# Attention loads placed nearer to their use, v loaded last, attention pairs moved over the slots, and one gather of gates moved to the first stretch

## The chip, the cores and the metric

One Trainium2 chip, of which the kernel uses one core. The time is the device time of that core in microseconds, median of several runs. A core has a matrix engine (TensorE, PE in the profile; its weight loads are PEld), a vector engine (DVE), a scalar engine (ACT), a GpSimd engine (POOL) and a sync engine (SP) that here does little else than issue transfers (DMAs). Each engine works through its own instructions in order. Where one needs what another makes, it waits on a semaphore, and all that is behind it on that engine waits too.

## The reference

Two blocks, one behind the other. The first is a linear attention with a decay `lam` for each head, over 4 batches, 8 heads, 768 positions and 64 values for each head:

```python
for b in range(nb):                                  # blocks along the sequence
    intra = einsum('bhic,bhjc->bhij', qb, kb) * Dmask[None]       # lam ** (i - j), lower triangle
    intra = einsum('bhij,bhjd->bhid', intra, vb)
    inter = einsum('bhid,bhde->bhie', qb * lam_pow[None], kv_state)
    out[:, :, sl] = intra + inter
    kb_dec = kb * rev_pow[None]
    kv_state = lam_block * kv_state + einsum('bhsd,bhse->bhde', kb_dec, vb)
```

Its output, as 3072 tokens of 512 values, is the input x of a mixture of four experts, whose gates come from another input:

```python
p = domain_probs / (domain_probs.sum(-1, keepdims=True) + 1e-09)
for e in range(E):                                   # E = 4, w1 is 512 x 1024, w2 is 1024 x 512
    h = np.maximum(x @ w1[e], 0.0)
    out += p[:, e:e + 1] * (h @ w2[e])
```

All is float32.

## The kernel before, in words

**Tiling.** The 3072 tokens are three groups, 0 to 2, of eight chunks of 128 tokens. A chunk is one batch's 128 positions with all heads. The attention works with chunks of 128 in place of the reference's blocks of 64, two chunks (a pair, n and n + 1) at a time, so a group has four pairs. Every expert product is a fast product with seven multiplications in place of eight, nested once more, so 7 x 7 small products; their sums and differences are made by DVE, POOL and ACT.

**One pair of attention** takes four steps:

- `load`: for each chunk q and k (two DMAs each, line 142) and v (one DMA, line 137) into buffers of 128 x 512. In groups 1 and 2 these come from the common pool of 41 small buffers; a new load waits until the last reader of its buffer is done.
- `turn`: q and k of a chunk are transposed by PE into the two accumulator banks s0 and s1, ACT copies them to qT and kT, and POOL multiplies k by a decay. For the last two chunks of each batch (the function `comes_across`; all of group 2's) q and k are laid out anew through DRAM before (`trickle`, `load_across`), and DVE transposes blocks in place, qx and then kx. That is work for the list `lately`, from which the loop takes one piece in each part.
- `scores` (line 581): products of kT and qT into four banks, sp. DVE multiplies them by the decay mask (`st <- sp, s_decay`, line 589) and, but for the first chunk, scales qT (`qT <- qT, q_decay`, line 593).
- `values` (lines 625, 631, 639): the product with the state, the product of the masked scores with v, and the new state. ACT copies the result, POOL makes the pair's sums for the fast product (`pair_sums`), and DVE updates the state.

**Order.** The order of the work is written out by hand; there is no search. Group 0's attention is done in the first stretch, up to 91.9 us, with parts of the first products put between its steps by the dictionary `between` (line 1325). The main loop then runs over 12 units (group, expert), each of 7 slots. A slot has 8 parts, 0 to 7, and carries one seventh of the second product of one unit and one seventh of the first product of the next. Slots are counted through from 0; slot s belongs to unit s // 7. Groups 1 and 2 are spread over these slots: `attention` (line 684) fills a list `steps` of (slot, part, work) from the table `AT`, which has one slot for each of the eight pairs. I count them from 1 to 8: pairs 1 to 4 are group 1, at slots 7, 10, 13 and 15; pairs 5 to 8 are group 2, at slots 22, 27, 32 and 37. The list is sorted by slot and part, and the loop takes out what is due at the end of each part (line 1496).

**Queues.** Nearly all DMAs are issued by SP in program order. In each slot these are the weights of the first product one slot ahead (`feed`, part 0, `ws_in`, two buffers), weights of the second product (`feed2`, `w2t`), stores of prepared sums, the attention's loads, and the blocks of x that a later group's products read (`x_fill`, part 3 of seven slots from `FILL[g]` on). POOL's work (`chores`) is taken from a list by an estimate of how busy POOL is: one chore when the estimated time of the last has gone by. DVE's smaller pieces wait in `background` and `lately`, one of each for a part.

**Gates.** `gates` (in the first stretch) turns the probabilities into gates for all tokens. The last group needs its gates along the other axis. `turn_gates`, a chore of unit (1, 0), gathers eight columns by eight DVE copies into a small tile gn (line 490), has PE transpose it (line 491, `gp`), and stores it to DRAM.

The lines that the prediction names beyond these: 899 is the matmul of the first product (`pg`), 953 that of the second (`q`), 812 the DMA of `feed`, 911 a relu by ACT, and line 101 is the helper `tt` through which DVE and POOL additions go, so that these are told apart by their tiles.

Of the kernel before, what the change touches and what calls it, by code (L numbers as in the profile page):

```python
# [14 lines left out]
FP32 = mybir.dt.float32  # L15
# [6 lines left out]
def kernel(  # L22
# [30 lines left out]
    nc = tc.nc  # L53

    B, H, S, D = q.shape
    E, DM, F = moe_w1.shape
    NTOK, DOUT = out.shape
    P = nc.NUM_PARTITIONS
# [3 lines left out]
    CPG = 8  # L62
# [8 lines left out]
    consts = ctx.enter_context(tc.tile_pool(name="consts", bufs=1))  # L71
# [16 lines left out]
    def bank(tag, name):  # L88
        return ps.tile([P, W], FP32, name=name, tag=tag)

    def small(name):
        return pool.tile([P, W], FP32, name=name, tag="t")
# [24 lines left out]
    def token(g, half, x):  # L117
        c, b = (half, x) if g == 0 else (2 * g + x % 2, 2 * (x // 2) + half)
        return b * S + c * C
# [4 lines left out]
    def where(n):  # L124
        g, x = divmod(n, CPG)
        return (x // 4, x % 4) if g == 0 else (2 * g + x // 2 % 2, 2 * (x // 4) + x % 2)
# [3 lines left out]
    def load(n, names="qkv"):  # L130

        c, b = where(n)
        for name in names:
            x = ({"k": acc_tile, "v": w2_tile} if n < CPG else {}).get(name, small)(f"{name}n")
            src = {"q": q, "k": k, "v": v}[name][b, :, c * C:(c + 1) * C, :]
            if name == "v":
                nc.sync.dma_start(out=x[:].rearrange("p (h d) -> p h d", d=D), in_=src.rearrange("h p d -> p h d"))
            else:
                to, of = x[:].rearrange("p (i r d) -> p i r d", r=2, d=D), src.rearrange("(r i) p d -> p i r d", r=2)
                for r in range(2):  # L140
                    by = nc.scalar if n < 2 and r == 1 else nc.sync
                    by.dma_start(out=to[:, :, r], in_=of[:, :, r])
            nat[n, name] = x[:].rearrange("p (h d) -> p h d", d=D)
# [202 lines left out]
    ident = consts.tile([P, P], FP32, name="ident")  # L346
# [42 lines left out]
    def trickle(m=1):  # L389
        for _ in range(m):  # L390
            if pieces:
                pieces.pop(0)[1]()

    def comes_across(n):
        return where(n)[0] >= SECOND

    def load_across(n):
        c, b = where(n)
        for x, name in enumerate("qk"):
            t = small(f"{name}x")  # L400
            nc.sync.dma_start(
                out=t[:].rearrange("p (h c) -> p h c", c=C),
                in_=across[x, :, :, b, (c - SECOND) * 4:(c - SECOND) * 4 + 4].rearrange("p h t d -> p h (t d)"),
            )
            nat[n, name + "x"] = t

    def load_more(n):
        if not comes_across(n):
            load(n)
        else:  # L410
            trickle(sum(b <= where(n)[1] for b, _ in pieces))
            load_across(n)
            load(n, "kv")

    lam_bc = consts.tile([P, H], FP32, name="lam_bc")
    nc.scalar.dma_start(out=lam_bc[:], in_=lam.partition_broadcast(P))
# [22 lines left out]
    for r in range(2):  # L439
        for ac in range(NHP):  # L440
            h = 4 * r + ac
            nc.vector.tensor_tensor_scan(
                out=s_decay[:, r, ac], data0=lam_bc[:, h:h + 1].to_broadcast([P, C]), data1=ident[:],
# [11 lines left out]
    while m < C:  # L455
        nc.vector.tensor_tensor(
            out=q_decay[:, :, m:2 * m], in0=q_decay[:, :, 0:m],
# [5 lines left out]
    kv = {b: small("kv") for b in range(0, B, 2)}  # L463
# [4 lines left out]

    probs = consts.tile([P, NTOK // P, E], FP32, name="probs")
    gate = consts.tile([P, NTOK // P, E], FP32, name="gate")  # L470


    gate_rows = dram.tile([CPG, E, P], FP32, name="gate_rows")
# [8 lines left out]
            out=gate[:], in0=probs[:], in1=total[:].unsqueeze(2).to_broadcast([P, NTOK // P, E]), op=ALU.mult,  # L482
        )

    def turn_gates():
        p, o, x = bank("s0", "gp"), small("gr"), small("gn")
        n = CPG * E
        for i in range(CPG):
            t = token(LAST, i // 4, i % 4) // P
            nc.vector.tensor_copy(out=x[:, i * E:(i + 1) * E], in_=gate[:, t])  # L490
        nc.tensor.transpose(out=p[0:n, 0:P], in_=x[:, 0:n], identity=ident[:])
        nc.scalar.copy(out=o[0:n, 0:P], in_=p[0:n, 0:P])
        nc.scalar.dma_start(out=gate_rows[:].rearrange("n e p -> (n e) p"), in_=o[0:n, 0:P])

# [3 lines left out]
    def hc(t):  # L498
        return t[:].rearrange("p (h c) -> p h c", c=C)
# [29 lines left out]
    def decayed(kn):  # L529

        kd = kn.rearrange("p (ac r) d -> p ac r d", r=2)
        by = k_decay.rearrange("p r ac -> p ac r").unsqueeze(3)
        tt(nc.gpsimd, kd, kd, by.to_broadcast([P, NHP, 2, D]), ALU.mult)

    def turn_across(n):

        qT, kT, kn = nat.pop((n, "qx")), nat.pop((n, "kx")), nat[n, "k"]

        def step(x):
            nc.vector.transpose(out=x[:], in_=x[:])  # L540
            if x is kT:
                turned[n] = qT, kT

        soon(n, *(lambda x=x: step(x) for x in (qT, kT)))
        if where(n)[0] < NCH - 1:
            decayed(kn)

    def turn(n, tags):
        if comes_across(n):
            turn_across(n)  # L550
            return
        qn, kn = nat.pop((n, "q")), nat[n, "k"]
        qp = bank(tags[0], "qp")
        kp = bank(tags[1], "kp")
        for x, y in ((qp, qn), (kp, kn)):
            for ac in range(NHP):
                nc.tensor.transpose(
                    out=x[:, ac * C:(ac + 1) * C], in_=y[:, 2 * ac:2 * ac + 2].rearrange("p r d -> p (r d)"),
                    identity=ident[:],
                )  # L560
        qT, kT = turned[n] = small("qT"), small("kT")
        nc.scalar.copy(out=qT[:], in_=qp[:])
        nc.scalar.copy(out=kT[:], in_=kp[:])
        if where(n)[0] < NCH - 1:
            decayed(kn)
# [3 lines left out]
    def scores(n, *tags):  # L569

        for m in (n, n + 1):
            while m not in turned:
                take(lately, True)
        masks, scale = [], []
        for m, pair in zip((n, n + 1), tags):
            qT, kT = turned.pop(m)
            scaled[m] = qT
            sp = [bank(pair[r], "sp") for r in range(2)]
            for ac in range(NHP):
                for r in range(2):  # L580
                    nc.tensor.matmul(  # L581
                        out=sp[r][:, ac * C:(ac + 1) * C], lhsT=hc(kT)[half[r], ac], rhs=hc(qT)[half[r], ac],
                        start=True, stop=True,
                    )
            del kT
            st = masked[m] = [small("st") for _ in range(2)]

            def mask(hd, st=st, sp=sp):
                tt(nc.vector, st[hd][:], sp[hd][:], s_decay[:, hd].rearrange("p h c -> p (h c)"), ALU.mult)

            masks.append([lambda hd=hd, mask=mask: mask(hd) for hd in range(2)])
            if where(m)[0]:
                scale.append(lambda qT=qT: tt(nc.vector, qT[:], qT[:], decay["q"][:], ALU.mult))
        if n < CPG:
            for f in masks[0] + masks[1] + scale:
                f()
        else:
            for f in masks[1]:
                f()
            soon(n, *masks[0], *scale)  # L600
# [76 lines left out]
            made.add(("blocks", g, x)),  # L677
        ))

    AT = 7, 10, 13, 15, 22, 27, 32, 37  # L680
    FILL = {1: 18, 2: 43}
    steps = []

    def attention(g):

        for n in range(g * CPG, (g + 1) * CPG, 2):
            at = AT[(n - CPG) // 2]
            steps.append((at - 2, 1, lambda n=n: load_more(n)))
            steps.append((at - 1, 1, lambda n=n: load_more(n + 1)))
            steps.append((at, 2, lambda n=n: turn(n, ("s0", "s1"))))  # L690
            steps.append((at, 5, lambda n=n: turn(n + 1, ("s0", "s1"))))
            steps.append((at, 7, lambda n=n: scores(n, ("s0", "s1"), ("g3", "g1"))))
            steps.append((at + 1, 7, lambda n=n: values(n, ("s0", "s1", "g3"))))
        steps.sort(key=lambda s: s[:2])
# [613 lines left out]
    m1, m2 = (direct_product(m, blocks, ("g1", "g3")) for m in ("M1", "M2"))  # L1308
    m5 = []

    def quarter_5(x):
        def step():
            if not m5:
                m5.extend(direct_product("M5", blocks, ("g1", "g3")))
            m5[x]()

        return step

    def step(*work):
# [4 lines left out]

    between = {
        1: ((m1[0], m1[2]), ()), 2: ((m2[0],), (m1[1], m1[3])), 3: ((m2[2],), (m2[1],)),
        4: ((m2[3],), (quarter_5(0), quarter_5(2))),
    }
    last_pair = CPG // 2 - 1
    for i in range(last_pair + 2):  # L1330
# [90 lines left out]
    for g in range(1, NG):  # L1421
        attention(g)
    PACE = 1.0, 1.4, 1.0
    for at, (g, e) in enumerate(units):
# [11 lines left out]
        for i in range(7):  # L1436
# [8 lines left out]
            if nests and i == 2:  # L1445
                nc.scalar.dma_start(
                    out=gate_bc, in_=gate_rows[:, ahead[1]].partition_broadcast(P),
# [25 lines left out]
            for x, part in enumerate(order):  # L1473
# [27 lines left out]
                for h in range(1, NG):  # L1501
                    if x == 3 and 0 <= at * 7 + i - FILL[h] < 7:
                        x_fill(h, SEQ[at * 7 + i - FILL[h]])
                pump(PACE[g])
# [30 lines left out]
```

## Time and profile before

| what | value |
|---|---|
| median of 3 runs | 1192.14 us (1192.09 to 1196.39) |
| the profiled execution | 1194.33 us |
| its span, first to last instruction | 1192.5 us |
| PE busy | 1172.8 us (98%), 6559 matmuls |
| DVE busy | 788.5 us (66%), 1323 instructions |
| POOL busy | 634.6 us (53%) |
| ACT busy | 263.8 us (22%) |
| mean granted clock of PE | 0.999 |
| DMA | 255.42 MB, 214 GB/s over the span |

Beside the busy times the profile has several views. The table of waits lists, for each engine and line, what it waited for, with the sum in us, the number of waits and the longest. The timeline lists instructions by start and duration, with the wait ahead of each in brackets. The view by stretches cuts the span at given times and sums each engine's busy time in each piece; its columns are the length, PE, PEld, DVE, ACT and POOL (each with its count), the granted clock, the busy share of the DMA engines and the GB/s. SPq is SP's issuing queue.

PE's longest pieces in the chain of work that ended last are the first products (37% of the span), the second products (29%) and the last group's nested products (13%).

### The profile page before, as it was taken

To read this page: it belongs to the slowest core of one execution; us is meant where nothing else is said; L and a number is where in the kernel's file an instruction comes from. 1 tells how busy PE (TensorE), PEld (TensorE's weight loads), DVE (VectorE), ACT (ScalarE), POOL (GpSimd) and SP (SyncE) were. 2 spreads that over 40 slices of the span, in tenths; PEclk is the share of its full clock that TensorE was granted. 3 is DMA by queue.
4 is the path that set the end of the run, shared out by engine and by line. 5 is a ranking of instruction groups with operands and counts; after the bars stand their busy time and mean duration, and the time that the engine had idled before them with its cause. 6 is when DMAs were issued, how large, how long until landed. Compare 5 with 4: busy or idle time off the path is not lost.

```text
span 1192.5 us, 17848 instructions
## 1 busy us (share of the span) xinstructions
PE 1172.8 (98%) x6559; PEld 1024.5 (86%) x6559; DVE 788.5 (66%) x1323; ACT 263.8 (22%) x464; POOL 634.6 (53%) x616
## 2 busy tenths in 40 slices
PE   9999999999979999999999999999999999999998
PEld 8888888888868888888888888888888888888887
DVE  4686884677367666737947754764775576777785
ACT  3221012112201201211220220121243342241331
POOL 2856166535555841034434414555695593783884
PEclk9999999999999999999999999999999999999999
DMA  9685578958896976659868656776774535444442
GB/s 232 191 256 186 160 228 277 284 191 273 268 351 215 288 244 211 198 181 284 262 208 251 211 191 211 252 245 209 242 237 167 178 132 186 141 158 169 144 183 71
DMA packets 264551, 255.42 MB, mean 214 GB/s; under 512 B 121200, under 2 KB 218256, under 8 KB 264464
## 3 DMA queue, kind: packets, MB, share of 16 engines
q1 hardware_dynamic: 253824, 251.46, 66.3%
q10 hardware_dynamic: 10640, 2.82, 1.0%
q8 instruction: 52, 0.85, 0.3%
q14 instruction: 35, 0.29, 0.1%
HBM read 180.80 MB, written 77.61 MB: 217 GB/s over the span
## 4 chain that ended last, share of the span: by engine, by line
PE 89%; DVE 7%; DMA 2%; POOL 1%; issue 0%; ACT 0%; SPq 0%; DVEq 0%; POOLq 0%
PE pg L899 37%; PE q L953 29%; PE pq L1179 13%; DVE m L101 3%; PE pM L1274 2%; PE op L631 2%; PE pc L1274 2%; DMA ws_in<-w_ops 1%; PE sp L581 1%; DVE st L101 1%; DVE qT L101 1%; PE op L625 1%; PE kvp L639 1%; POOL acc L101 0%; POOL m L101 0%
## 5 line engine op out<-in xcount | busy, mean ns | idle before, releaser
L899 PE MATMUL pg<-xs,ws_in 128*128 128x256 f32 x1960 | 471.4, 381 | 9.0 <-DVE m L101 4.9
L899 PEld LDWEIGHTS pg<-xs,ws_in 128*128 128x128 f32 x1960 | 372.1, 191 | 63.2 <-DVE m L101 8.4
L953 PE MATMUL q<-w2t,m 128*128 128x256 f32 x1792 | 425.3, 380 | 0.0
L953 PEld LDWEIGHTS q<-w2t,m 128*128 128x128 f32 x1792 | 338.8, 190 | 47.5 <-DVE m L101 0.4
L101 DVE TENSOR_TENSOR m<-pg,m 128x512 f32<-128x512 f32 x451 | 307.1, 687 | 105.4 <-PE pg L899 97.5
L969 DVE SCALAR_TENSOR_TENSOR acc<-q,gate,acc 128x256 f32<-128x256 f32 x192 | 92.4, 481 | 138.9 <-PE q L953 138.1
L101 DVE TENSOR_TENSOR m<-m,m 128x512 f32<-128x512 f32 x184 | 151.7, 824 | 9.8 <-ACT m L911 9.8
L911 ACT ACTIVATE m<-m 128x512 f32<-128x512 f32 x132 | 82.9, 630 | 291.0 <-DVE m L101 290.7
L101 POOL TENSOR_TENSOR m<-m,s_decay 128x512 f32<-128x512 f32 x64 | 81.9, 1297 | 58.7 <-ACT m L911 45.5
L101 DVE TENSOR_TENSOR sums<-pq,sums 128x256 f32<-128x256 f32 x153 | 64.2, 422 | 45.7 <-PE pq L1179 36.9
L907 ACT COPY m<-pg 128x512 f32<-128x512 f32 x88 | 51.5, 587 | 183.9 <-PE pg L899 175.6
L101 POOL TENSOR_TENSOR xs<-xs 128x256 f32<-128x256 f32 x56 | 44.2, 789 | 86.6 <-DMA xs<-x_blocks 70.7
L1179 PE MATMUL pq<-acc,w2t 128*128 128x256 f32 x352 | 86.6, 379 | 0.0
L101 POOL TENSOR_TENSOR to<-xc 128x256 f32<-128x256 f32 x16 | 13.2, 825 | 129.1 <-ACT xc L651 91.1
L1179 PEld LDWEIGHTS pq<-acc,w2t 128*128 128x128 f32 x352 | 66.8, 190 | 9.3 <-issue 0.3
L101 POOL TENSOR_TENSOR w2o<-w2b 128x512 f32<-128x512 f32 x32 | 41.9, 1330 | 37.0 <-DMA w_sums<-w2o 18.6
L840 ACT ACTIVATE m<-m 128x512 f32<-128x512 f32 x44 | 27.7, 630 | 134.4 <-DVE m L101 134.4
L101 POOL TENSOR_TENSOR acc<-hT,hT 128x512 f32<-128x512 f32 x32 | 40.3, 1273 | 29.3 <-PE pq L1179 27.4
L101 POOL TENSOR_TENSOR ops<-w2b 128x256 f32<-128x256 f32 x24 | 18.3, 785 | 56.5 <-DMA w2b<-in_moe_w_dram 56.5
L101 POOL TENSOR_TENSOR acc<-hT,acc 128x512 f32<-128x512 f32 x32 | 40.7, 1272 | 7.7 <-PE pq L1179 5.7
L101 DVE TENSOR_TENSOR st<-sp,s_decay 128x512 f32<-128x512 f32 x48 | 30.4, 682 | 17.8 <-PE sp L581 17.8
L101 POOL TENSOR_TENSOR w1o<-w1b 128x512 f32<-128x512 f32 x20 | 27.5, 1400 | 22.5 <-DMA w_ops<-ops 9.9
(128 smaller groups left out, 1190.5 us busy)
## 6 DMA issues: line engine op xcount, KB each, us to landing
ws_in<-w_ops SPq DMA_DIRECT2D x70, 896.0 KB, 6.4
w2t<-w_ops SPq DMA_DIRECT2D x66, 256.0 KB, 5.0
w2t<-w_sums SPq DMA_DIRECT2D x64, 256.0 KB, 3.3
w_ops<-ops SPq DMA_DIRECT2D x28, 512.0 KB, 3.9
w2t<-in_moe_w_dram SPq DMA_DIRECT2D x48, 256.0 KB, 3.2
w2b<-in_moe_w_dram SPq DMA_DIRECT2D x32, 256.0 KB, 6.1
w_sums<-w2o SPq DMA_DIRECT2D x16, 512.0 KB, 5.0
w2b<-in_moe_w_dram SPq DMA_DIRECT2D x16, 512.0 KB, 8.0
```

Of the source, the lines that this page charges most:

```text
L101: eng.tensor_tensor(out=o, in0=a, in1=b, op=op)
L581: nc.tensor.matmul(out=sp[r][:, ac * C:(ac + 1) * C], lhsT=hc(kT)[half[r], ac], rhs=hc(qT)[half[r], ac], start=True, stop=True,)
L625: nc.tensor.matmul(out=place(i, a, r, x), lhsT=state_of[half[r], i, 2 * a + x], rhs=hc(qs[m])[half[r], 2 * a + x], start=(i == 0 and a == ...
L631: nc.tensor.matmul(out=place(i, a, r, x), lhsT=vn[m][:, 4 * r + 2 * a + x], rhs=hc(st[m][r])[:, 2 * a + x], start=(first and i == 0 and a ...
L840: nc.scalar.activation(out=o[:], in_=o[:], func=AF.Relu)
L899: nc.tensor.matmul(out=p[:, j * 256:(j + 1) * 256], lhsT=ws[i][:, j * P:(j + 1) * P], rhs=xs[i], start=(fresh and j == 0), stop=True, skip ...
L907: nc.scalar.copy(out=new[at][:], in_=p[:])
L911: nc.scalar.activation(out=new[at][:], in_=new[at][:], func=AF.Relu)
L953: nc.tensor.matmul(out=p[:, s * DH:(s + 1) * DH], lhsT=h[A_OF[m]][:, c * 256 + s * P:c * 256 + (s + 1) * P], rhs=fed2[g, e, m][uu][:, c], ...
L969: nc.vector.scalar_tensor_tensor(out=o, in0=x, scalar=w, in1=o, op0=ALU.mult, op1=ALU.add)
L1179: nc.tensor.matmul(out=p[:, 0:256], lhsT=fed3[e, m, x // 2][:, x % 2, c * P:(c + 1) * P], rhs=b[B_OF[i]][:, c * 256:(c + 1) * 256], start= ...
L1274: nc.tensor.matmul(out=p[:, s * 256:(s + 1) * 256], lhsT=a[c][:, f:f + P], rhs=b[:, c, j * 256:(j + 1) * 256], start=(s == 0 and c == 0 an ...
```

## The change

Four things. In the order of `attention`, a chunk's q and k are loaded in the slot ahead of the transposes (parts 3 and 7), where they came one or two slots ahead (part 1), and v no longer goes with them: both v tiles are loaded one slot after the transposes, in part 1 of the slot whose part 7 has the values. The second chunk's transposes move from part 5 to part 6. Second, the pairs' slots in `AT` change, and group 1's x blocks start one slot earlier (17 for 18). Third, the eight copies of the last group's gates move from `turn_gates` into `gates`, into a tile of their own. Fourth, in the first stretch a pair's scalings come before its masks, and the two pieces of products put around the last pair's step change places.

```diff
--- before
+++ after
@@ -406,11 +406,11 @@
 
     def load_more(n):
         if not comes_across(n):
-            load(n)
+            load(n, "qk")
         else:
             trickle(sum(b <= where(n)[1] for b, _ in pieces))
             load_across(n)
-            load(n, "kv")
+            load(n, "k")
 
     lam_bc = consts.tile([P, H], FP32, name="lam_bc")
     nc.scalar.dma_start(out=lam_bc[:], in_=lam.partition_broadcast(P))
@@ -468,6 +468,7 @@
 
     probs = consts.tile([P, NTOK // P, E], FP32, name="probs")
     gate = consts.tile([P, NTOK // P, E], FP32, name="gate")
+    last_gate = consts.tile([P, CPG * E], FP32, name="last_gate")
 
 
     gate_rows = dram.tile([CPG, E, P], FP32, name="gate_rows")
@@ -482,13 +483,14 @@
             out=gate[:], in0=probs[:], in1=total[:].unsqueeze(2).to_broadcast([P, NTOK // P, E]), op=ALU.mult,
         )
 
-    def turn_gates():
-        p, o, x = bank("s0", "gp"), small("gr"), small("gn")
-        n = CPG * E
         for i in range(CPG):
             t = token(LAST, i // 4, i % 4) // P
-            nc.vector.tensor_copy(out=x[:, i * E:(i + 1) * E], in_=gate[:, t])
-        nc.tensor.transpose(out=p[0:n, 0:P], in_=x[:, 0:n], identity=ident[:])
+            nc.vector.tensor_copy(out=last_gate[:, i * E:(i + 1) * E], in_=gate[:, t])
+
+    def turn_gates():
+        p, o = bank("s0", "gp"), small("gr")
+        n = CPG * E
+        nc.tensor.transpose(out=p[0:n, 0:P], in_=last_gate[:], identity=ident[:])
         nc.scalar.copy(out=o[0:n, 0:P], in_=p[0:n, 0:P])
         nc.scalar.dma_start(out=gate_rows[:].rearrange("n e p -> (n e) p"), in_=o[0:n, 0:P])
 
@@ -592,7 +594,7 @@
             if where(m)[0]:
                 scale.append(lambda qT=qT: tt(nc.vector, qT[:], qT[:], decay["q"][:], ALU.mult))
         if n < CPG:
-            for f in masks[0] + masks[1] + scale:
+            for f in scale + masks[0] + masks[1]:
                 f()
         else:
             for f in masks[1]:
@@ -677,18 +679,19 @@
             made.add(("blocks", g, x)),
         ))
 
-    AT = 7, 10, 13, 15, 22, 27, 32, 37
-    FILL = {1: 18, 2: 43}
+    AT = 5, 8, 11, 14, 22, 27, 33, 36
+    FILL = {1: 17, 2: 43}
     steps = []
 
     def attention(g):
 
         for n in range(g * CPG, (g + 1) * CPG, 2):
             at = AT[(n - CPG) // 2]
-            steps.append((at - 2, 1, lambda n=n: load_more(n)))
-            steps.append((at - 1, 1, lambda n=n: load_more(n + 1)))
+            steps.append((at - 1, 3, lambda n=n: load_more(n)))
+            steps.append((at - 1, 7, lambda n=n: load_more(n + 1)))
             steps.append((at, 2, lambda n=n: turn(n, ("s0", "s1"))))
-            steps.append((at, 5, lambda n=n: turn(n + 1, ("s0", "s1"))))
+            steps.append((at, 6, lambda n=n: turn(n + 1, ("s0", "s1"))))
+            steps.append((at + 1, 1, lambda n=n: (load(n, "v"), load(n + 1, "v"))))
             steps.append((at, 7, lambda n=n: scores(n, ("s0", "s1"), ("g3", "g1"))))
             steps.append((at + 1, 7, lambda n=n: values(n, ("s0", "s1", "g3"))))
         steps.sort(key=lambda s: s[:2])
@@ -1324,7 +1327,7 @@
 
     between = {
         1: ((m1[0], m1[2]), ()), 2: ((m2[0],), (m1[1], m1[3])), 3: ((m2[2],), (m2[1],)),
-        4: ((m2[3],), (quarter_5(0), quarter_5(2))),
+        4: ((quarter_5(0), quarter_5(2)), (m2[3],)),
     }
     last_pair = CPG // 2 - 1
     for i in range(last_pair + 2):
```

## The prediction

> **What bounds the kernel now.** I read the busy shares first, then TensorE's waits, then the stretches between them.
>
> ```profile
> PE 1172.8 (98%) x6559; PEld 1024.5 (86%) x6559; DVE 788.5 (66%) x1323; ACT 263.8 (22%) x464; POOL 634.6 (53%) x616
> ```
>
> TensorE (PE) sets the time: 19.7 us of the 1192.5 us span are idle, a few of them at both ends. The instruction counts of the changed kernel are the same, so it can only win or lose waits of PE. PE's waits, by releaser:
>
> ```profile
> PE pg L899 <- DVE m L101: 5.1, 4, 2.8
> PE pg L899 <- DMA ws_in<-w_ops: 3.2, 1, 3.2
> PE gp L491 <- DVE gn L490: 1.8, 1, 1.8
> PE op L625 <- DVE qT L101: 1.4, 2, 0.9
> ```
>
> Where? From 91.9 us the main loop runs in slots (7 per unit). A slot takes 12.95 us (91.9 to 104.85); with the values of a pair at its end 17.0 (slot 8). Three slots of group 1's attention, out of the table by stretches (PE busy, weight loads, DVE, ACT, POOL, clock, DMA share), beside slot 8:
>
> ```profile
> 198.30:215.30 17.00, 17.00 (x157) 14.93 (x157) 8.38 (x14) 3.40 (x6) 3.92 (x4) 1.00 0.95 293
> ...
> 245.10:264.10 19.00, 17.52 (x159) 14.75 (x157) 15.77 (x24) 1.64 (x3) 9.09 (x9) 1.00 0.36 119
> ...
> 294.00:311.80 17.80, 17.23 (x157) 14.84 (x157) 8.98 (x15) 2.34 (x4) 15.77 (x18) 1.00 0.90 274
> ...
> 328.60:353.80 25.20, 19.17 (x159) 15.96 (x157) 17.42 (x23) 1.04 (x2) 11.23 (x9) 0.93 1.00 352
> ```
>
> The same work, so slots 11, 14 and 16 lose 2.0, 0.8 and 8.2 us: 11.0. In slot 11 the DMA share is 0.36, because the SP queue stood still; its waits between 240 and 265 us, and its timeline:
>
> ```profile
> SPq L142 <- PE op L625: 8.1, 1, 8.1
> SPq L142 <- DVE qT L101: 7.2, 1, 7.2
> ```
> ```profile
> 245.26 0.34 SPq L812 DMA_DIRECT2D ws_in<-w_ops  x1
> 260.94 0.92 SPq L142 DMA_DIRECT2D qn<-in_q_dram  x2
> ...
> 309.10 3.50 SPq L142 DMA_DIRECT2D kn<-in_k_dram  x2
> 313.04 2.20 SPq L137 DMA_DIRECT2D vn<-in_v_dram  x1
> ...
> 326.35 0.42 SPq L812 DMA_DIRECT2D ws_in<-w_ops  x1
> ```
>
> A q load, put early in slot 11, takes a buffer that pair 2's values free only at that slot's end. Behind it 15 us of transfers pile up; SP then issues without a pause from 286 us, and the weights of slot 16 leave at 326.35. They land 7.33 us later, PE idles 3.2, and the clock falls to 0.83 (330 to 340 us; 24 matmuls in 6.79 us where 5.2 is usual: 1.6 more). The rest of slot 16 is DVE:
>
> ```profile
> 338.02 1.68 DVE L101 TENSOR_TENSOR m<-m,m 128x512 f32<-128x512 f32 x1
> ...
> 339.11 6.73 POOL L101 TENSOR_TENSOR w2o<-w2b,w2o 128x512 f32<-128x512 f32 x4
> ...
> 339.62 1.75 DVE L101 TENSOR_TENSOR qT<-qT,q_decay 128x512 f32<-128x512 f32 x1
> ```
>
> Beside POOL an addition of two SBUF tiles takes 1.7 us; alone it takes 0.68 (its steps are 0.60 apart). PE then waits 2.8 us for an accumulator.
>
> [...]
>
> **The change, part by part.** The built order of instructions shows what moves; no time is taken from it.
>
> *Pairs 3 and 4, loads later, v apart.* q and k of a pair are now issued in the slot before the transposes. Pair 3's first load sits in slot 10 and waits for pair 2's values, now at slot 9's end: that is past, and no other load of this group waits for something that is still to come. The hole in SP's queue goes, and with it the pile. What SP has to issue per slot: q and k 4.7 us when the engines are busy (1.62 + 3.12 at 291 us), v 2.2, the rest of a slot 6 to 10; slot 13, with two loads, comes to some 17 us (estimate from these), so its weights leave 4 us into slot 14, land 7.6 later, and are due at 17. Slot 16's transfer wait and slow clock (4.8) go, and the DVE stalls of slots 11, 14 and 16 move with the pairs: gain 11.0.
>
> *Where the DVE stalls go.* A pair's masks and scalings (6 operations, 3.6 us) now fall into slots 6, 9, 12, 15 instead of 8, 11, 14, 16. Slot 15 (4.7 us of DVE work now) is empty enough: 0. Slot 6 (7.9 of 13): 0.3. Slot 9 gets the DVE sequence that slot 16 has now, 12.4 us uncontended; POOL's w2 sums lie near it: between 0 and 2.8, I take 1.0. Slot 12 has 14.2 us uncontended: 4 masks, 2 scalings, 4 gated additions of 0.40, 15 others of 0.60. Slot 33 does as much now (14.6 us) and PE doesn't wait; but POOL makes w1 sums in slot 12. Between 0 and 5; I take slot 11's 2.0.
>
> *Later transposes of a pair's second chunk (part 5 to 6), group 2.* The transposition of kx now stands directly before the masks. In slot 27 DVE has these before it:
>
> ```profile
> 504.17 0.65 DVE L101 TENSOR_TENSOR m<-pg,m 128x512 f32<-128x512 f32 x1
> ...
> 504.85 0.63 ACT L911 ACTIVATE m<-m 128x512 f32<-128x512 f32 x1 [2.08 <-DVE m L101]
> ...
> 505.51 0.69 DVE L101 TENSOR_TENSOR m<-m,m 128x512 f32<-128x512 f32 x1 [0.70 <-ACT m L911]
> ```
>
> kx ends at 506.1 + 0.7 = 506.8; the second half of the scores is due at 503.89 + 1.0 = 504.9: a new wait of 1.9 on PE, with everything queued behind it. In slot 33 five operations (0.4 + 4 x 0.6), then kx, end 3.7 after the last q product, due at 1.95: 1.7. In slots 22 and 36 no other operation lies between: 0. Pair 8's masks go from slot 38 to 37: 0.3.
>
> *Gates gathered early.* The eight copies (0.66 us) leave slot 28, where PE's transposition waits 1.84: gain 1.8. They go to about 80 us, where DVE is 79% busy and PE always; hidden by PE's products, 0.66 at most.
>
> *First stretch.* With the scalings first, a pair's masks are 1.2 to 2.8 us later (two scalings beside POOL took 2.77). There the second pair's masks free the bank that the next transposes need: PE loses about 1.25 there. The last pair's scalings and the two products put before its values cover 1.42 of waiting, and some 0.45 that the table hides: gain 0.6.
>
> *x blocks one slot earlier, pairs 7 and 8 moved:* same transfers, first used four slots (52 us) later: 0; without that cover one transfer, 6.2.
>
> Sum: -11.0 - 0.6 - 1.8 + 0.3 + 1.0 + 2.0 + 1.9 + 1.7 + 0.3 = -6.2. The profiled execution took 1194.33 (1192.5 span and 1.8 around it): 1188.1. It lies 2.2 above the median of the runs, 1192.14; there the same difference gives 1185.9.
>
> **Rivals.** B, *DVE becomes the bound of slots 9 and 12*: POOL works through both. For it speaks slot 16 (2.8 us of PE waiting with fewer additions), against it slot 33. With 2.8 and 5.0 the sum is -1.4: 1190.7, no change. C, *slower: v is late*. It is issued a part into the slot and used six parts later, 9.7 us plus 1.1 of state products. Two issues of 2.2 and 4.9 of landing take 9.3. If SP is more than 1.5 us behind there, PE waits at the values; 3 us behind at all eight pairs would cost 12 and give 1198. For it: SP was 11 us behind at 326; against it: the hole that made it so is gone. D, *the hole stays*: another load waits for values of its own slot; then only gates and first stretch count, about 1193. The buffers as built speak against it.
>
> **How the numbers follow.** My forecast 0.50, B 0.30, D 0.08, C 0.12. Faster means by over 0.5%, about what a measurement of this kernel can tell from no change: under 1186.2; slower is over 1198.1. The forecast lies just inside; I count its own range (1179 to 1188, from no collisions in DVE at all, 13.4 of gain, to 1 us more each in slots 9 and 12) nearly wholly as faster, since slot 9's and 12's costs may be nothing: faster 0.50, same 0.38, slower 0.12. The range that holds 8 in 10 runs from 1179 to 1195: B with one more late transfer like slot 16's (4.8) ends it.
>
> **What would show it.** Right: DMA share near 0.9 in slots 9 to 11, no wait of PE for ws_in, 17 us in slot 15; new idle time of PE before the scores of slots 27 and 33, released by kx; none before gp. Wrong: PE waiting for vn at the values (C); a load blocked for over 5 us on SP (D); slot 12 over 20 us (B).

## The result and the profile after

The changed kernel takes 1195.72 us (median of 20 runs, 1194.04 to 1202.66), the kernel before 1192.18 in as many (1190.88 to 1196.45). The ratio is 1.0028, with a 95% interval of 1.0016 to 1.0039: by the medians 3.5 us slower, where 6 us of gain were forecast, and above the top of the range. Run once more beside three of the experiments it was 1.0033 (1.0020 to 1.0046).

The profiled execution took 1194.96 us. It lies 0.8 below its median, while the one of before lay 2.2 above its own, so the two profiles differ by 0.6 us only. That alone warns against reading the two profiles as the two kernels.

Busy shares of the changed kernel, and then its table of waits for PE (sum in us, number, longest):

```profile
PE 1172.2 (98%) x6559; PEld 1024.6 (86%) x6559; DVE 791.0 (66%) x1323; ACT 264.6 (22%) x464; POOL 631.1 (53%) x616
```
```profile
PE pg L902 <- DVE m L101: 4.1, 3, 2.3
PE sp L583 <- issue: 3.6, 2, 1.9
PE qp L559 <- issue: 2.2, 1, 2.2
PE qp L559 <- DMA qn<-in_q_dram: 2.0, 2, 1.2
PE kp L559 <- DMA kn<-in_k_dram: 1.1, 2, 0.6
```

The waits for `ws_in` and for gn are gone, as forecast, and the scores wait 3.6 us, as forecast. The last three lines stand in the first stretch: a wait of 2.2 ahead of the last pair's transposes, where 1.25 was in the sum, and 3.1 for loads, which were in no sum. The view by stretches (columns as before) of slots 9, 12, 15, 16 and 34:

```profile
223.35:242.91 19.56, 17.27 (x158) 14.84 (x156) 16.24 (x23) 0.99 (x2) 9.68 (x7) 1.00 0.92 280
272.75:291.25 18.50, 17.27 (x159) 14.84 (x157) 17.48 (x26) 5.63 (x10) 11.90 (x12) 1.00 0.90 265
321.08:338.09 17.01, 17.01 (x158) 14.94 (x156) 8.38 (x14) 3.33 (x6) 4.86 (x5) 1.00 0.98 299
338.09:351.15 13.06, 13.06 (x65) 11.51 (x62) 10.39 (x15) 0.09 (x1) 8.76 (x8) 1.00 0.84 289
590.54:609.24 18.70, 18.70 (x158) 16.12 (x157) 12.07 (x20) 3.51 (x6) 0.33 (x1) 0.91 0.49 146
```

Slot 9 takes 19.56 (17.0 without a loss), slot 12 18.50, slot 15 17.01. Slot 16, which took 25.20 before with a pair's values in it, has no values now and loses nothing. Slot 34 is the odd one: PE is busy throughout, and yet it takes 18.70, because the clock was granted at 0.91 (at 0.50 for 3.41 us, from 591.05). Between 150 and 360 us SP's longest wait at a q or k load is now 1.1 (8.1 before); PE never waits for vn:

```profile
SPq L142 <- PE pg L902: 1.3, 2, 1.1
SPq L142 <- DVE acc L972: 1.1, 1, 1.1
SPq L142 <- DMA ws_in<-w_ops: 1.0, 2, 0.7
```

And slot 27, in the timeline of PE, DVE and ACT:

```profile
500.93 1.16 PE L583 MATMUL sp<-qx,kx 64*128 64x128 f32 x16
501.20 0.65 DVE L101 TENSOR_TENSOR m<-pg,m 128x512 f32<-128x512 f32 x1
501.89 0.63 ACT L914 ACTIVATE m<-m 128x512 f32<-128x512 f32 x1 [2.09 <-DVE m L101]
502.55 0.69 DVE L101 TENSOR_TENSOR m<-m,m 128x512 f32<-128x512 f32 x1 [0.69 <-ACT m L914]
...
503.15 0.70 DVE L542 STREAM_TRANSPOSE kx<-kx 128x512 f32<-128x512 f32 x1
...
503.96 0.79 PE L583 MATMUL sp<-qx,kx 64*128 64x128 f32 x9 [1.87 <-issue]
```

The transposition of kx stands behind the addition that waits for a relu, and the second half of the scores waits 1.87 us for it. The releaser is given as "issue", but the matmuls begin 0.1 us after kx ends.

Where did the time go, slot for slot? The slots are cut at the first matmul of each second product. From the start of the main loop to the start of slot 20, and from profile to profile (five kernels that have the old slots and loads, seven that have the new ones, the experiments below among them):

| us | old slots and loads | new slots and loads |
|---|---|---|
| slots 0 to 19 | 302.7, 301.0, 300.9, 300.0, 299.3 | 298.4, 298.4, 297.7, 297.7, 297.5, 297.2, 295.6 |
| slots 11 + 14 + 16 over 3 x 17.0 | 11.0, 9.2, 8.6, 8.3, 7.4 | none |
| slot 9 over 17.0 | none | 5.4, 5.4, 4.7, 4.6, 4.5, 4.2, 2.6 |
| slot 12 over 17.0 | none | 1.5 in all |

The profile of before that I read (302.7) was the worst of its five, and that of the changed kernel (295.6) the best of its seven. Between them lie 7.1 us, between the medians 3.2.

### The profile page after: what moved, and what is told of

Its sections match the earlier page's. It is cut to its first block, busy times and chain, and to the rows that moved or that the text cites. A ratio compares the mean times of both kernels' runs of the same rounds, so it can differ in the third digit from the quotient of the medians.

```text
span 1193.1 us, 17863 instructions
## 1 busy us (share of the span) xinstructions
PE 1172.2 (98%) x6559; PEld 1024.6 (86%) x6559; DVE 791.0 (66%) x1323; ACT 264.6 (22%) x464; POOL 631.1 (53%) x616
## 4 chain that ended last, share of the span: by engine, by line
PE 91%; DVE 4%; SPq 1%; DMA 1%; POOL 1%; issue 1%; ACT 0%; ACTq 0%; POOLq 0%; DVEq 0%
PE pg L902 38%; PE q L956 31%; PE pq L1182 13%; PE pM L1277 2%; PE op L633 2%; PE pc L1277 2%; DVE m L101 2%; PE sp L583 2%; PE op L627 1%; SPq L142 1%; PE kvp L641 1%; DVE qT L101 1%; POOL acc L101 0%; POOL m L101 0%; DVE st L101 0%
## 5 line engine op out<-in xcount | busy, mean ns | idle before, releaser
L101 POOL TENSOR_TENSOR to<-xc 128x256 f32<-128x256 f32 x16 | 11.7, 728 | 144.6 <-ACT xc L653 141.1
L101 POOL TENSOR_TENSOR kn<-kn,s_decay 128x512 f32<-128x512 f32 x20 | 21.9, 1097 | 56.2 <-PE kp L559 43.6
```

The costliest lines, as they stand in the source:

```text
L101: eng.tensor_tensor(out=o, in0=a, in1=b, op=op)
```

## The experiments

All were timed in five rounds beside the kernel before, 5 to 22 runs of each, in four groups; in these before had 1193.74, 1192.71, 1193.60 and 1194.19 us. Ratios are to the before of the same group, with the 95% interval. Differences in us are those of the medians, unless the text says that they come from the ratios; the two ways can lie 1 us apart.

**The first stretch's order, alone.**

```diff
-            for f in masks[0] + masks[1] + scale:
+            for f in scale + masks[0] + masks[1]:
-        4: ((m2[3],), (quarter_5(0), quarter_5(2))),
+        4: ((quarter_5(0), quarter_5(2)), (m2[3],)),
```

> The kernel before with the first stretch's part alone: scalings ahead of masks, and the two pieces around the last pair exchanged. Theory 1 (late masks): the second chunk's transposes of the last pair wait for the masks of the pair before, as in the changed kernel's profile (2.2 us ahead of qp at 42 us), and 1.4 us of waits at the values shrink to 0.8; the main loop starts 1.7 us later and the time is 1.5 to 2 us above before. Rival (slow first transfers): the order costs nothing net (-0.6 to 0.3 us) and the changed kernel's late start came from its first loads alone.

1193.98 us, 0.9997 (0.9982 to 1.0013): the time doesn't resolve it. The trace does. PE in the first stretch:

```profile
39.08 0.63 PE L557 MATMUL qp<-ident,qn 128*128 128x128 f32 x4 [1.75 <-issue]
54.27 0.44 PE L625 MATMUL op<-qT,kv 64*64 64x128 f32 x4 [0.82 <-DVE st L101]
54.87 1.09 PE L625 MATMUL op<-qT,kv 64*64 64x128 f32 x28 [0.16 <-DVE st L101]
```

The transposes wait 1.75 us, and the main loop begins at 91.63 where before begins at 89.99: 1.64 later. As a figure for the kernel this is rough: two of the experiments below that leave the first stretch as it was (the attention's part alone, and the new loads alone) begin at 91.3 and 91.4, held up by late loads. The wait itself is firm; all six profiles with the scalings first have it, from 1.75 to 2.3 us, and no other has more than 0.5 us of it.

**The masks first again, in the changed kernel** (the exchange of the two pieces stays).

```diff
-            for f in scale + masks[0] + masks[1]:
+            for f in masks[0] + masks[1] + scale:
```

> The changed kernel with the masks ahead of the scalings again, but with the two pieces around the last pair still exchanged. Theory 1: the wait of 2.2 us ahead of the last pair's transposes is gone, and the exchanged piece covers the waits at the last pair's values; the main loop starts 2 to 3 us earlier than in the changed kernel, 2 to 3 us less time. Rival (the exchange helps only together with the scalings first): the waits of 1.4 us at the values come back and no more than 1 us is gained.

1194.44 us, 1.0009 (0.9993 to 1.0024), against 1.0033 of the changed kernel in the next group. The wait ahead of the transposes is gone, the last pair's values don't wait at all, and the main loop begins at 92.23 in place of 94.44. So the order of masks and scalings costs some 2 us here, though the intervals of the two ratios still overlap a little, and the exchange of the two pieces does its work without that order.

**The second chunk's transposes in part 5 again, in the changed kernel.**

```diff
-            steps.append((at, 6, lambda n=n: turn(n + 1, ("s0", "s1"))))
+            steps.append((at, 5, lambda n=n: turn(n + 1, ("s0", "s1"))))
```

> The changed kernel with the second chunk's transposes in part 5 again. Theory 1 (kx late): the two waits of 1.9 and 1.7 us ahead of the scores in slots 27 and 33 go, with the slow clock behind the second (1.8 us): 3.5 to 5.5 us less than the changed kernel. Rival (the vector engine is full there, kx only shows it): the wait moves to an accumulator one or two parts later and less than 1.5 us is gained.

1192.28 us, 0.9989 (0.9973 to 1.0006). The wait of slot 27 is gone (15.11 us for the slot in place of 17.17), that of slot 33 falls from 1.74 to 0.63, and slots 33 and 34 take 33.5 us together in place of 35.7. (In the second profile of the changed kernel, without a slow clock in slot 34, the two take 34.05.) Against the 1.0033 of the changed kernel that is some 5 us.

**The gates' part, alone.** The diff is the one of the change.

> The kernel before with the gates gathered in the first stretch alone. Theory 1: the wait of 1.8 us ahead of gp goes and nothing comes for it: 1.8 us less than before. Rival: the eight copies at about 80 us stop an addition in front of the main loop, and the gain is under 1 us; a rival for the start of the changed kernel is that the new constant tile, which shifts the buffers behind it, makes the first transfers 2 us later here too.

1194.09 us, 0.9999 (0.9983 to 1.0014). The wait of 1.84 ahead of gp is gone, and the main loop begins at 92.36, 2.4 later than in before. This start was the riddle. The four profiles with the new tile (the changed kernel and three experiments) waited for the fifth chunk's or its neighbour's loads at 26 to 28 us; the two without it did not. In the built program `last_gate` takes 128 bytes of each partition, ahead of all work buffers: these begin at multiples of 512 bytes in before, and 128 bytes past such a multiple in the changed kernel. The rows of q, k and v are packets of 256 bytes. Of the packets of that size in the first 40 us of the trace (24576), at most 0.2% take over 25 ns where the buffers stand at multiples of 512, and 12 to 17% where they are shifted (means 18.0 and 20.2 to 21.2 ns; 0.2% and 18.0 in before, 14% and 20.5 in the changed kernel). What moved is the destination in SBUF; why a packet takes longer there was not shown. Three experiments below are on this alone.

**The changed kernel itself once more**, as their base.

> The changed kernel itself once more, as the base beside the three others. Both theories: the main loop starts at 94 to 96 us, the waits of 1.9 and 1.7 us stand ahead of the scores of slots 27 and 33, and the time is 2 to 4 us above before; second and third pair's scores of the first stretch are 14.6 us apart, where before has 12.6.

1197.34 us, 1.0033 (1.0020 to 1.0046). Slot 9 of this execution, by stretches:

```profile
224.23:245.87 21.64, 18.96 (x158) 16.04 (x156) 16.73 (x23) 0.98 (x2) 7.89 (x6) 0.92 0.82 250
```

PE is idle for 2.7 us in it, and then the clock falls (0.92): 4.6 us in place of the 2.6 of the first profile.

**The tile of gates 512 bytes wide**, in the changed kernel.

```diff
-    last_gate = consts.tile([P, CPG * E], FP32, name="last_gate")
+    last_gate = consts.tile([P, P], FP32, name="last_gate")[:, 0:CPG * E]
```

> The changed kernel with the new tile of gates made 512 bytes wide in each partition in place of 128, of which the first 128 are used; every buffer behind it starts at a multiple of 512 bytes again. Theory 1 (shifted buffers): the rows of 256 bytes of the first loads land at addresses 128 bytes past a multiple of 256 in the changed kernel and are slow for it. The share of such packets that take over 25 ns falls from some 14% to under 1%, second and third pair's scores stand 12.6 us apart in place of 14.6, and the kernel takes 2 to 3 us less than the changed one. Rival (chance of the run): the loads are as slow as in the changed kernel, and nothing is gained.

1194.00 us, 1.0002 (0.9989 to 1.0015): 3.3 below the changed kernel beside it. 0.2% of the packets are slow again. PE still waits 1.2 us for loads at 26 us in this profile, so the spacing of 12.6 us that I had named didn't come (14.2). Late loads are thus not the shift's alone: in the first stretch PE waits 1.6 to 3.1 us for q and k in the seven profiles with shifted buffers, and in the nine with unshifted ones nothing in five and 0.5 to 1.8 us in four. The third pair's scores begin at 36.2 to 38.6 us in the seven, and at 34.1 to 35.7 in the nine.

**128 unused bytes ahead of the buffers, in the kernel before, and nothing else.**

```diff
+    consts.tile([P, CPG * E], FP32, name="pad")
```

> The kernel before with an unused tile of 128 bytes in each partition ahead of its buffers, and nothing else. Theory 1 (shifted buffers): second and third pair's scores stand 14.5 us apart in place of 12.6, the main loop starts some 2 us later, and the time is 2 us above before. Rival (the eight copies, or chance): the times of before, main loop at 90 us.

1196.10 us, 1.0021 (1.0008 to 1.0035): 3.4 above before (2.5 by the ratio), with not one instruction changed. The DMA view of the first 40 us (issues, KB, median us from issue to landing), first of before, then of this:

```profile
vn<-in_v_dram SPq DMA_DIRECT2D x8, 256.0 KB, 4.3
qn<-in_q_dram SPq DMA_DIRECT2D x14, 128.0 KB, 4.0
kn<-in_k_dram SPq DMA_DIRECT2D x14, 128.0 KB, 3.8
```
```profile
vn<-in_v_dram SPq DMA_DIRECT2D x8, 256.0 KB, 5.2
qn<-in_q_dram SPq DMA_DIRECT2D x14, 128.0 KB, 4.4
kn<-in_k_dram SPq DMA_DIRECT2D x14, 128.0 KB, 4.2
```

And PE at the transposes that come too early for them:

```profile
26.86 0.63 PE L558 MATMUL qp<-ident,qn 128*128 128x128 f32 x4 [1.25 <-DMA qn<-in_q_dram]
27.78 0.63 PE L558 MATMUL kp<-ident,kn 128*128 128x128 f32 x4 [0.30 <-DMA kn<-in_k_dram]
```

The place of the buffers is shown to be the cause of the slow packets, and of some 3 us of the time, in both directions. No offset but 128 bytes was tried. After the first stretch the effect is smaller: from 100 to 400 us the packets of 256 bytes take 18.4 ns in the changed kernel and 18.0 in before. With the old loads it stays larger (19.2 and 19.5 ns in the two kernels that have them and shifted buffers), but their slots 0 to 19, at 299.3 and 300.0 us, are the shortest of the five old ones.

**The gates' part with the wide tile**, in the kernel before.

> The kernel before with the gates gathered in the first stretch alone, in a tile 512 bytes wide, so that no other buffer's place against multiples of 512 bytes moves. Theory 1 (two opposite effects in the gates' part): first loads as fast as in before, no wait of 1.8 us ahead of gp: 1 to 2.5 us less than before, where the narrow tile gave 0.3 us more. Rival (the eight copies cost as much as they save): within 0.5 us of before.

1192.03 us, 0.9983 (0.9969 to 0.9996), 2 us below before. The main loop begins at 90.10, and PE waits 0.2 ahead of gp in place of 1.84. The idea of this part was worth what the sum said; in its narrow form, 128 bytes took it back.

**The attention's slots, loads and x blocks, alone** in the kernel before.

> The kernel before with the new slots, loads and transposes of the attention and the x blocks one slot earlier, but with its own first stretch and gates. Theory 1: the main loop starts as in before; slots 0 to 20 gain 6 to 8 us; of this 1.9 us go at the scores of slot 27 and 3.5 at those of slot 33 with the slow clock behind it; 1 to 3 us less than before. Rival (the gain in the slots is an accident of one execution): less than 3 us are gained up to slot 20, and the kernel is 2 us or more slower than before.

1195.03 us, 1.0014 (1.0001 to 1.0026). Slots 0 to 19 take 298.4 us, 1 to 4 less than in the profiles of the old ones. Slots 27 and 33 lose 1.87 and 1.74, slot 34 runs at a slow clock again (slots 33 and 34 take 35.7 us). The gain up to slot 19 is real, but some 3 us by the medians where 7.7 were forecast, and the scores with the slow clock behind them take more than that back.

**The new slots with the old loads and transposes**, and **the old slots with the new loads**, in the kernel before.

```diff
-    AT = 7, 10, 13, 15, 22, 27, 32, 37
-    FILL = {1: 18, 2: 43}
+    AT = 5, 8, 11, 14, 22, 27, 33, 36
+    FILL = {1: 17, 2: 43}
```

> The kernel before with the new slots of the pairs and the x blocks one slot earlier, but all loads and transposes placed as before. Theory 1 (the loads' place made the hole in the sync engine's queue): a load waits some 8 us or more for the values of the pair ahead, and PE waits again for the weights two or more slots later; slots 0 to 19 take 299 to 302 us as in before. Rival (the slots of the pairs did it): no wait for weights, 297 to 298 us as in the changed kernel. No waits ahead of the scores of slots 27 and 33 in either.

> The kernel before with the loads and transposes placed as in the changed kernel, but the pairs at their old slots. Theory 1 (loads): no wait of PE for weights and no load that waits over 3 us; the vector engine's stalls of slots 11 and 16 stay (2 and 3 us); slots 0 to 19 take 296 to 298 us, less than the 299 to 302 of before, and waits of 1.9 us stand ahead of the scores of group 2's pairs where additions come before kx. Rival (slots): slots 0 to 19 take 299 us or more.

The new slots alone: 1190.99 us, 0.9973 (0.9957 to 0.9989). The new loads alone: 1196.52, 1.0021 (1.0011 to 1.0032). With the new slots a load still blocks SP for 8.1 us, as SP's waits show,

```profile
SPq L142 <- PE q L953: 8.1, 1, 8.1
```

and yet PE waits for no weights up to slot 22 (once for 1.5 us in slot 23), and slots 0 to 19 take 295.3 us. There the first theory fell: the hole in SP's queue is no loss by itself. Even with the old slots it doesn't always make weights late: of the five profiles that have both, four wait 2.3 to 4.6 us for them, and the gates' part alone, whose load blocks SP for 10.9 us, not at all. With the old slots and no hole, slots 0 to 19 take 296.1, and no weights are late either. So no late weights up to slot 19 were seen where either the hole or the old slots were gone. But the new loads bring the later transposes along, and three pairs of group 2 wait at their scores:

```profile
501.32 1.21 PE L581 MATMUL sp<-qx,kx 64*128 64x128 f32 x16 [1.87 <-issue]
...
576.92 1.16 PE L581 MATMUL sp<-qx,kx 64*128 64x128 f32 x16 [1.33 <-issue]
...
649.82 1.16 PE L581 MATMUL sp<-qx,kx 64*128 64x128 f32 x16 [1.63 <-issue]
```

**Three repairs in the changed kernel**: the wide tile, the masks first, and the transposes in part 5, for group 2 in part 4.

> The changed kernel with three repairs: the tile of gates 512 bytes wide, the masks ahead of the scalings in the first stretch (the two pieces around the last pair stay exchanged), and the second chunk's transposes in part 5 (group 1) and part 4 (group 2). Theory 1 (each repair is worth what it was alone): 2 to 3 us from the first loads, 2 us from the masks, 4 to 5 us from the scores of slots 27 and 33; 8 to 9 us below the changed kernel and some 4 us below before. Slot 9 still loses 4 to 5 us. Rival (the repairs overlap, since a later start hides waits): 4 us or less below the changed kernel, no gain over before.

1188.44 us, 0.9955 (0.9938 to 0.9972), from five runs. By the ratios some 9 us below the changed kernel, near the sum of the single ones (3.3 + 2 + 5).

**With a pair's scalings later, besides.** They were given to the vector engine one after the other behind the masks.

```diff
-            soon(n, *masks[0], *scale)
+            soon(n, *masks[0], *(after(4 + x, f) for x, f in enumerate(scale)))
```

> The kernel of the three repairs with a pair's two scalings given to the vector engine four and five parts after its scores, in groups 1 and 2. Theory 1 (the burst of masks and scalings in slot 9 makes an accumulator late): the wait of 2.3 to 3.5 us in slot 9 and the slow clock behind it go, slot 9 takes 17 to 19 us in place of 21 to 22, and 2 to 4 us are gained over the three repairs. Rival (the vector engine is full in slot 9, 16.2 us of work beside GpSimd): the wait moves to a later part and less than 1 us is gained.

1181.87 us, 0.9900 (0.9883 to 0.9917), from five runs: 11.7 below before, the fastest kernel here. Slots 9 and 12, by stretches, and its longest waits of PE:

```profile
218.29:236.13 17.84, 17.28 (x158) 14.86 (x156) 15.49 (x23) 0.98 (x2) 8.69 (x7) 1.00 0.95 291
265.97:283.44 17.47, 17.28 (x158) 14.86 (x156) 17.21 (x26) 5.40 (x10) 12.47 (x13) 1.00 0.84 244
```
```profile
PE op L633 <- DVE st L101: 1.5, 2, 1.3
PE zp L430 <- DVE zeros L425: 1.1, 1, 1.1
PE pg L902 <- DVE m L101: 1.0, 3, 0.6
```

DVE's work in slot 9 is nearly the same (15.5 us for the 16.6 of the three repairs, where the slot took 21.48), so it was not full: two scalings in the midst of the additions that free PE's accumulators made it late. There, beside POOL, they took 1.75 us each; four and five parts later they take 0.68. One of the two in slot 9, in the changed kernel and then in this one:

```profile
228.78 1.75 DVE L101 TENSOR_TENSOR qT<-qT,q_decay 128x512 f32<-128x512 f32 x1
```
```profile
228.88 0.68 DVE L101 TENSOR_TENSOR qT<-qT,q_decay 128x512 f32<-128x512 f32 x1
```

**The later scalings alone, in the changed kernel.**

> The changed kernel with only a pair's scalings given to the vector engine four and five parts after its scores, in groups 1 and 2. Theory 1 (slot 9's burst): slot 9 falls from 20 to 22 us to 17 to 19, slot 12 by 1 us, and the kernel is 4 to 6 us below the changed one, at 1190 to 1193 us; the misplaced buffers, the late masks of the first stretch and kx in slots 27 and 33 stay. Rival (only together with the other repairs): 2 us or less.

1190.51 us, 0.9971 (0.9960 to 0.9982), with slot 9 at 18.6 and slot 12 at 17.0 us; slot 23, which no expectation names, takes 17.0 too, where the seven profiles without this have 17.0 to 18.4. The buffers, the late masks and kx are all still there, and this one line turns a loss of 0.33% into a gain of 0.29%.

## Why the prediction was wrong

Its terms, with what the runs showed (us; minus is a gain):

| term | forecast | measured |
|---|---|---|
| slots 11, 14, 16 | -11.0 | -8.6 (median of five profiles, 7.4 to 11.0) |
| slot 6 / 9 / 12 / 15 | +0.3 / +1.0 / +2.0 / 0 | 0 / +4.6 / +1.5 / 0 |
| scores of slot 27 | +1.9 | +1.9 |
| scores of slot 33 | +1.7 | +1.7, and 0 or 1.7 of slow clock behind it |
| pair 8's masks (slots 36 to 38) | +0.3 | +0.2 |
| gates: wait ahead of gp | -1.8 | -2.0 (time of the wide tile; -1.7 in slot 28) |
| first stretch, order | -0.6 | +1.6 (one pair of profiles) |
| rest of slots 0 to 20 (x blocks earlier among it) | 0 | -1.0 |
| place of the buffers | not seen | +3.3 |

The measured column makes +3.2, and +4.9 with 1.7 for the clock behind slot 33; the medians show 3.5 and 4.6 in the two comparisons. The spread of single runs doesn't allow a closer check. Put into the kernel before one by one, the first stretch, the gates and the attention's part have 0.9997, 0.9999 and 1.0014, which multiply to 1.0010 where the whole has 1.0028 and 1.0033; the intervals leave room for that, and for some effect of the parts on each other.

*The largest error, and the one step that wasn't in the sum at all, is the place of the buffers.* "Gates gathered early" counted eight copies, a wait and no more. The part also adds a tile, and a tile ahead of all pools moves every buffer. That could have been asked before any run: the tile's size stands in the diff, 32 values of 4 bytes, and in the first stretch of before the loads come just in time. None of the rivals had it. It doesn't make the wrong sign alone: without it the changed kernel stands at 1.0002, no gain yet, and with it, but with the pairs' scalings later, at 0.9971. The gain of 6.2 was used up by four terms together: the buffers (3.3 us worse than forecast), slots 9 and 12 (3.1), slots 11, 14 and 16 (2.4) and the first stretch (2.2). The forecast rival for "slower", C, was wrong: v was never late. D's 1193 doesn't follow from its own two terms, which give -2.4 and so 1189.7.

*"First stretch" had the right wait with the wrong size and a cover too large.* The bank freed late was forecast to cost 1.25 and cost 1.75 to 2.3; it is freed by the third pair's masks, not the second's, since the first two pairs have no scalings. In two of six profiles a slow clock of 1.7 us followed. On the other side 1.42 of waiting and 0.45 hidden were to be covered; 0.2 to 1.0 of waiting stayed at the values, since the masks were now what came last. What covered the values was the exchange of the two pieces, and that needed no change in the order of masks (with the masks first, no wait at the values in one profile and 0.5 us in another).

*"Pairs 3 and 4": the loss was there, its mechanism only in part, and the 11.0 was one execution's.* The sum took the loss of slot 16 as a property of the kernel. In five profiles the three slots lose from 7.4 to 11.0. The hole was read as the cause of the late weights; the new slots alone, hole and all, had none late there, nor had one of the five with hole and old slots. Late weights up to slot 19 were seen only where both came together, and not always then. (Of the 15 us that SP stood still, the DMA engines moved nothing in 9, from 252 to 261 us: DMA share 0.00, 0 GB/s.)

*"Where the DVE stalls go": slot 9 was priced at 1.0 and costs 4.6.* Rival B was right that DVE is late there beside POOL, and 2.8 was its price for the wait: 2.3 to 3.5 were measured. What neither had is the slow clock behind such a wait, another 1.7 us in six of seven profiles (none in the changed kernel's own), though the profile of before had shown one in slot 16. B's 5.0 for slot 12 was too much.

*"Later transposes, group 2" was right to 0.1 us* for the two waits, again without the clock.

## What to carry to other kernels

Ask of every new tile where it puts the others: 128 bytes ahead of the pools cost 3.3 us here, as much as the attention's new slots gained alone. A wait on the bounding engine has to be priced with the slow clock that may follow it (1.7 us each time here), and a loss read from one execution as one draw. When a stall moves, look at the order in the queue before the sum of work: two operations of each pair, four and five parts later, were worth some 7 us, more than twice what the new slots gained.

## What was not expected of the hardware

- Packets of 256 bytes into buffers 128 bytes past a multiple of 512: 12 to 17% of them took over 25 ns in the first 40 us (0.2% otherwise), and loads landed 0.4 to 0.9 us later.
- The slow clock came in one size. In the main loop and the first stretch of the sixteen profiles it was granted at a half 19 times, each time for 3.41 us (from 333.65 us in before and from 591.05 in the changed kernel, where the view by stretches gives 0.50), so each cost 1.7 us, however long the wait before it. These waits were 1.6 to 3.5 us long, and the same wait had a slow clock behind it in some executions and none in others: two of five after the 1.74 us in slot 33 (8 matmuls in 3.31 us there, 1.89 usual; a sixth profile waits 2.43 and has one), two of seven after the 1.87 in slot 27, and the 2.29 in slot 9 had none in the changed kernel and one with the masks first. What decides it was not tried.
- The runs' times went with their mean clock: before had medians of 1191.2 us at 1.000 (34 of 75 runs), 1194.8 at 0.999 and 1196.0 at 0.997. Of 42 runs of the changed kernel one had 1.000 (the rest 0.993 to 0.999), and of the fastest kernel's five all five.
